# An mLSTM kernel with a gated MLP behind it: how the first four cells get their decay matrices, and the order of the head around it

## The chip, the cores and the metric

The kernel runs on one core of a Trainium2 chip. A core has a matrix engine (TensorE, PE in the profile; its weight loads are listed apart as PEld), a vector engine (VectorE, DVE), a scalar engine for activations (ScalarE, ACT), a general engine (GpSimd, POOL) and a queue that only issues transfers (SyncE, SP). Each takes its instructions in the written order and waits on semaphores for the others. The metric is the time of one execution in device microseconds (us), and less is better.

## The reference

The first block is an mLSTM cell: 4 batches by 8 heads, 768 steps, head size 40. Per step, with a running maximum `m` that keeps the exponentials in bounds:

```python
m_new = np.maximum(f_gate[:, :, t] + m, i_gate[:, :, t])
f_stab = np.exp(f_gate[:, :, t] + m - m_new)
i_stab = np.exp(i_gate[:, :, t] - m_new)
C = f_stab * C + i_stab * np.einsum('bhd,bhe->bhde', vt, kt)
n = f_stab * n + i_stab * kt
y[:, :, t] = sigmoid(o_gate) * (C @ qt) / np.maximum(np.abs(n @ qt), 1.0)
```

Its output (3072 rows of 320) goes through an MLP: `h = x @ w_in` (320 by 2048), `g = h * cos(h)`, `out = g @ w_out`. All inputs are float64 in memory, so the kernel also turns the bits of the weights into float32.

## The kernel before

**Tiling.** The sequence is cut into six chunks of 128 steps. One cell is one chunk of one batch (8 heads), so there are 24 cells; cell n is chunk n // 4 of batch n % 4. Within a cell the recurrence is done as attention: the scores of q and k are weighted with a decay matrix E[s, h, t] = exp(a_s - M_t), zero for s > t, where F is the running sum of the forget gates, a = i - F and M the running maximum of a. The weighted scores times the values give the outputs, and what the chunk leaves for later ones is added to a state. The MLP of a chunk (its four cells are its 512 columns) runs while the next chunk's cells are made.

**Stages.** `first_cells` is the head: the gates, cells 0 to 3, the gates of the other five chunks (32 rows by 640), and the preparation of cell 4 (B = 4). `first_period` starts the MLP of chunk 0 with `Up(0, 0)`: two weight rows of the first dimensions (L749) and the last 64 dimensions (`low`, L743), then scores and values of cell 4. After it the matrix engine has the MLP's products and one cell per period to the end. The order of all of it is written out by hand (`manual_schedule`): the calls in `first_cells` are the order of each engine's queue.

**A cell of the head.** `turn` transposes q and k on PE, `turn_out` copies them from PSUM on ACT, `scores` multiplies them, `weigh` multiplies the scores with E on DVE (two halves, L566), `values` multiplies with the values on PE, `normalize` divides on DVE (L650 to L658), `seam` transposes the result and makes the state's increment on PE, `seam_out` copies the transposed output (xT, L712) and `state` the increment (L724) on ACT.

**E in the head.** The maxima M are split into three bfloat16 parts (`maxima_in_parts`: five DVE instructions, L271 to L275, and one ACT copy) so that a bfloat16 product can spread them over all partitions. `maxima_in` puts into a PSUM bank a wall (1e30 where s > t, `wall_in`, L442, 128x512) and adds M with four products per half cell (`spread`, L449). `less_sums` subtracts a on DVE, in two halves per cell (L467), into E; `decay` takes exp(-E) on ACT (L472, 128x1024).

**The later gates.** `gates_sums` is a DVE scan over 640 columns (L290), `gates_less_sums` subtracts on POOL (L293 to L295), `gates_maxima` is the second DVE scan (L298) and sends M to memory from POOL's queue (L300, M_d), `gates_shifts` makes m0 on POOL (L304, L305). `gates_carry` takes five exponentials on ACT, one per chunk with the bias m0 (L309), and sends them from POOL's queue in two transfers (L312, G_d). `gates_exp` takes five more with the bias -M of the chunk's end (L316). `gates_turn` and `gates_turn_out` put a and these exponentials into a table by partition (`tab`).

**Weights.** `take_apart` (two ACT instructions, L175 and L177), `bound` (two on DVE, L181 and L182), `join` (DVE, L191) and `round_up` (POOL, L196) turn a piece of float64 bits into float32. Cell 4's E comes back from M_d (`load_M`, L436), is walled by POOL's `decay_exponents` (L462) and goes through eight exponentials (L476). `weigh_k` (POOL, L481) weights k for the state; `odd_constants` are four POOL memsets (L138, L139). `warm` (L1096) issues matmuls of zeros into a bank that nobody reads.

Of the kernel before, what the change touches and what calls it, by code (L numbers as in the profile page):

```python
# [29 lines left out]
def kernel(  # L30
# [57 lines left out]
    M0_parts = small[:, 704:768].bitcast(BF)  # L88
    of_parts = small[:, 768:784].bitcast(BF)
    nc.vector.memset(nil, 0.0)  # L90
    ident = const.tile([128, 128], FP, name="ident")
# [8 lines left out]
    nc.vector.memset(M0_parts, 0.0)  # L100
    nc.vector.memset(of_parts, 0.0)

    nc.gpsimd.memset(wall, 0.0)
# [163 lines left out]
    def maxima_in_parts():  # L267
# [8 lines left out]
        nc.scalar.copy(out=M0_parts[BH:2 * BH], in_=mid)  # L276

    def gates_first_out():
        pg = ps_o.tile([128, 2, BH], FP, name="pg", tag="o")
        for j, src in enumerate((a0, e0)):  # L280
            nc.tensor.transpose(pg[:, j], src, ident[0:BH, 0:BH])
        nc.vector.tensor_copy(out=tab[:, 0, 0:2], in_=pg)
# [24 lines left out]
    def gates_carry():  # L307
        for c in range(R):
            nc.scalar.activation(out=eG[:, c], in_=M1[:, c], func=AF.Exp, scale=-1.0, bias=m0[:, c:c + 1])  # L309
        dst = G_d.rearrange("(c j q) s -> j q c s", c=R, j=2)  # L310
        for j in range(2):
            nc.gpsimd.dma_start(out=dst[j], in_=eG[j:BH:2])  # L312

    def gates_exp():
        for c in range(R):
            nc.scalar.activation(out=eW[:, c], in_=a1[:, c], func=AF.Exp, bias=nM1[:, c:c + 1])  # L316

# [134 lines left out]
    def psum_o():  # L452
        return ps_o.tile([128, HP, C], FP, name="pm", tag="o")
# [15 lines left out]
    def decay(n, heads=range(H)):  # L469
        c, b = divmod(n, B)  # L470
        if n < B:
            nc.scalar.activation(out=Es[n], in_=Es[n], func=AF.Exp, scale=-1.0)  # L472
            return
# [634 lines left out]
    def first_cells():  # L1108
# [40 lines left out]
        turn_out(1, False)  # L1149
        weigh(0)  # L1150
        sigmoid_next()
        sigmoid(0)
        exp_next()
        gates_sums()
        gates_less_sums()
        values(0)
        pieces.extend(weights_in(0))
        scores(1)
        weigh(1)
        maxima_in(2)  # L1160
        less_sums(2)
        decay(2)
        values(1)
        normalize(0)
        normalize(1)
        maxima_in(3)
        less_sums(3)
        turn(2)
        turn_out(2, False)
        weigh_k(2)  # L1170
        seam(0)
        seam_out(0)
        scores(2)
        state(0)
        decay(3)
        weigh(2)
        seam(1)
        seam_out(1)
        weigh_k(3)
        gates_maxima()  # L1180
        gates_shifts()
        load_M(B)
        load_blocks(B)
        load(B, "kv")
        outs.append((0, weights_out(0)))
        turn(3)
        turn_out(3, False)
        values(2)
        normalize(2)
        state(1)  # L1190
# [43 lines left out]
        decay(B)  # L1234
        odd_constants()
        odd_values_of(B)
# [418 lines left out]
```

## Time and profile before

| what | us |
|---|---|
| median of 3 runs | 505.82 |
| lowest, highest | 504.16, 506.86 |
| the profiled execution | 503.72 |
| its span in the profile | 501.9 |
| PE busy | 495.1 |
| DVE busy | 420.6 |
| ACT busy | 332.5 |
| POOL busy | 300.0 |

A line of the timeline has the start in us from the span's start, the busy time, the engine, the line of the kernel, the operation with output and inputs, its shape, and a count; in brackets is the idle time before it and what ended that. A line by source shows the shortest, median and longest duration in ns.

### The profile page before, as it was taken

The page shows a single profiled execution, that of the slowest core. Times are in us where ns is not written, and L with a number is a line of the kernel's source. Part 1 is how long each engine was busy: PE and PEld are TensorE (multiplying, and loading weights), DVE is VectorE, ACT ScalarE, POOL GpSimd, SP SyncE. Part 2 cuts the span into 40 slices and gives each one's busy share as a digit, 9 for nine tenths or more (in the row PEclk, how much of TensorE's full clock was granted, in tenths as well). Part 3 has the DMA queues.
Part 4 walks back from the last instruction along what each step waited for, and adds up shares of the span by engine and source line. Part 5 has one row for each costly group of instructions (what it writes and reads, how often), then busy time and mean ns, then how long its engine had stood idle before and what let it go on. Part 6 is the DMA issues. An engine that isn't in the chain of part 4 may idle for free.

```text
span 501.9 us, 11143 instructions
## 1 busy us (share of the span) xinstructions
PE 495.1 (99%) x4038; PEld 375.4 (75%) x4038; DVE 420.6 (84%) x842; ACT 332.5 (66%) x646; POOL 300.0 (60%) x394
## 2 busy tenths in 40 slices
PE   9999999999999999999999999999999999999997
PEld 6856656565667668887887888788788888787876
DVE  7899998999878878899889889889979866777565
ACT  6799997878564575765877846777847743443541
POOL 8254557666555576787558877657567446434340
PEclk9999999999999999999999999999999999999999
DMA  9989899997366346129446118628113000010001
GB/s 139 182 223 239 213 224 279 233 217 136 114 178 111 101 120 127 50 86 202 132 125 106 48 54 195 168 83 150 43 35 85 1 7 5 2 54 0 2 0 54
DMA packets 100663, 56.74 MB, mean 113 GB/s; under 512 B 63456, under 2 KB 93360, under 8 KB 100608
## 3 DMA queue, kind: packets, MB, share of 16 engines
q1 hardware_dynamic: 97408, 54.43, 46.8%
q10 hardware_dynamic: 2896, 1.23, 1.0%
q8 instruction: 32, 0.52, 0.5%
q0 software_dynamic: 304, 0.36, 0.3%
q14 instruction: 23, 0.19, 0.1%
HBM read 50.66 MB, written 4.10 MB: 109 GB/s over the span
## 4 chain that ended last, share of the span: by engine, by line
PE 85%; ACT 4%; DVE 3%; DMA 2%; SPq 2%; POOL 2%; issue 1%; DVEq 0%; ACTq 0%; POOLq 0%
PE acc L1014 24%; PE pup L817 17%; PE pup L749 9%; PE po L863 6%; PE pup L833 6%; PE late L1014 5%; PE ps L560 4%; PE pup L743 3%; PE vt L595 2%; PE vt L586 2%; PE pu L701 2%; PE ph L576 1%; DMA E<-M_d 1%; DMA vs<-in_v_dram 1%; DVE n L760 1%
## 5 line engine op out<-in xcount | busy, mean ns | idle before, releaser
L757 ACT ACTIVATE n<-pup 128x512 int32<-128x512 f32 x64 | 37.0, 593 | 84.2 <-DVE pup L842 58.4
L765 ACT ACTIVATE n<-n 128x512 f32<-128x512 f32 x96 | 57.7, 626 | 16.5 <-DVE n L760 12.5
L852 POOL TENSOR_TENSOR g<-g,n 128x512 f32<-128x512 f32 x31 | 39.6, 1278 | 47.5 <-ACT n L765 47.4
L749 PE MATMUL pup<-xT,w_in_sb 128*128 128x512 f32 x128 | 58.7, 601 | 0.3 <-ACT xT L712 0.2
L1014 PE MATMUL acc<-w_out_sb,g 128*128 128x160 f32 x320 | 58.7, 303 | 0.0
L760 DVE SCALAR_TENSOR_TENSOR n<-pup,n 128x512 f32<-128x512 f32 x64 | 43.1, 689 | 18.5 <-ACT n L757 15.9
L834 POOL TENSOR_TENSOR blocks<-blocks 128x256 f32<-128x256 f32 x32 | 25.1, 785 | 54.5 <-ACT blocks L826 54.5
L1014 PE MATMUL acc<-T,g 128*128 128x160 f32 x304 | 56.4, 301 | 0.0
L817 PE MATMUL pup<-xT,w_in_sb 128*128 128x256 f32 x192 | 53.5, 385 | 0.2
L476 ACT ACTIVATE E<-E,tab 128x128 f32<-128x128 f32 x160 | 50.1, 389 | 4.3 <-POOL E L462 4.1
L1014 PEld LDWEIGHTS acc<-w_out_sb,g 128*128 128x128 f32 x320 | 49.0, 190 | 4.7 <-issue 2.7
L769 DVE TENSOR_TENSOR g<-pup,n 128x512 f32<-128x512 f32 x64 | 42.7, 687 | 5.7 <-ACT n L765 4.8
L1014 PEld LDWEIGHTS acc<-T,g 128*128 128x128 f32 x304 | 46.5, 190 | 1.1 <-issue 0.4
L749 PEld LDWEIGHTS pup<-xT,w_in_sb 128*128 128x128 f32 x128 | 23.1, 189 | 30.7 <-issue 30.0
L825 ACT COPY blocks<-pup 128x512 f32<-128x512 f32 x32 | 18.6, 582 | 34.2 <-PE pup L817 33.8
L817 PEld LDWEIGHTS pup<-xT,w_in_sb 128*128 128x128 f32 x192 | 33.8, 189 | 9.6 <-ACT blocks L826 4.4
L817 PE MATMUL pup<-x_room,room 128*128 128x256 f32 x128 | 38.5, 382 | 0.0
L542 POOL TENSOR_TENSOR qG<-t,G 128x512 f32<-128x512 f32 x20 | 26.4, 1321 | 16.7 <-DVE t L538 16.7
L1014 PE MATMUL acc<-T,blocks 128*128 128x160 f32 x160 | 36.2, 308 | 0.2 <-POOL blocks L904 0.2
L863 PE MATMUL po<-w_out_sb,g 128*128 128x320 f32 x128 | 36.2, 436 | 0.1
L833 PE MATMUL pup<-xL,w_in_l 64*128 64x512 f32 x128 | 36.1, 641 | 0.0
L566 DVE TENSOR_TENSOR E<-ps,E 128x512 f32<-128x512 f32 x46 | 29.5, 682 | 5.8 <-PE ps L560 5.6
(227 smaller groups left out, 1210.7 us busy)
## 6 DMA issues: line engine op xcount, KB each, us to landing
E<-M_d SPq DMA_DIRECT2D x20, 512.0 KB, 6.0
qr<-in_q_dram SPq DMA_DIRECT2D x72, 80.0 KB, 2.6
kr<-in_k_dram SPq DMA_DIRECT2D x72, 80.0 KB, 2.2
bits<-in_moe_w_out_dram SPq DMA_DIRECT2D x8, 640.0 KB, 6.2
G<-G_d SPq DMA_DIRECT2D x18, 256.0 KB, 5.7
blocks<-in_moe_w_in_dram SPq DMA_DIRECT2D x32, 128.0 KB, 4.6
out_dram<-o_sb SPq DMA_DIRECT2D x23, 160.0 KB, 1.8
o<-in_o_gate_dram SPq DMA_DIRECT2D x40, 80.0 KB, 4.4
```

Of the source, the lines that this page charges most:

```text
L476: nc.scalar.activation(out=Es[n][:, h], in_=Es[n][:, h], func=AF.Exp, scale=-1.0, bias=tab[:, c, 0, g:g + 1])
L566: nc.vector.tensor_tensor(out=w, in0=pss[n][j], in1=w, op=OP.mult)
L749: nc.tensor.matmul(pu.rearrange("p (b t) -> p b t", b=B), w_in_sb[:, i, ts(2 * f2 + e, 128)], xT[c][:, i:NK * B:NK], start=(i == 0 and not ...
L757: nc.scalar.activation(out=self.n[e], in_=self.pu[e], func=AF.Copy, bias=0.25)
L760: nc.vector.scalar_tensor_tensor(out=self.n[e].bitcast(FP), in0=self.pu[e], scalar=0.25, in1=self.n[e], op0=OP.add, op1=OP.subtract)
L765: nc.scalar.activation(out=r, in_=r, func=AF.Sin, scale=TWO_PI_DOWN)
L769: nc.vector.tensor_tensor(out=g, in0=self.pu[e], in1=self.n[e].bitcast(FP), op=OP.mult)
L817: nc.tensor.matmul(bank[:, part].rearrange("p (b t) -> p b t", b=B // 2), w[:, f2], x, start=start, stop=stop, skip_group_check=True)
L833: nc.tensor.matmul(pu, w_in_l[r, f2], xL[c][r].rearrange("p b t -> p (b t)"), start=False, stop=True, skip_group_check=True)
L852: tt(out=self.g, in0=self.g, in1=self.n[e].bitcast(FP), op=OP.mult)
L863: nc.tensor.matmul(po[c][b], gs[c, f][:, ts(b, C)], w_out_sb[:, f], start=(f == 0), stop=(f == NF - 1))
L1014: nc.tensor.matmul(a, lhs, rhs, start=start, stop=stop)
```

## The change

For cells 2 and 3 the DVE subtraction goes. A new `sums_in_parts` splits -a into three bfloat16 parts as M is split already, and `exponents_in` puts a into the bank by a product (128x512) in the place of the wall; M is added as before. ACT takes the exponential straight from PSUM in two halves, and POOL zeroes s > t behind it (128x1024). `gates_carry` and `gates_exp` become a POOL subtraction or addition over all 640 columns and one exponential each. The order of the head changes: `gates_maxima` ahead of `weigh(2)`, `scores(2)` and the turn of cell 3 ahead of `seam(1)`, the first `take_apart` ahead of `state(0)`, `values(2)` behind `scores(3)`, `load_M` of cell 4 behind four other loads, `odd_constants` early; two calls of `warm` (8 matmuls) go.

```diff
+    a0_parts = small[:, 784:848].bitcast(BF)
+    nc.vector.memset(a0_parts, 0.0)
...
+    def sums_in_parts():
+        rest, mid = blocks[0:BH, 38], blocks[0:BH, 39].bitcast(BF)[:, 0:C]
+        hi = a0_parts[0:BH]
+        nc.vector.tensor_scalar(out=hi, in0=a0, scalar1=-1.0, scalar2=None, op0=OP.mult)
+        nc.vector.scalar_tensor_tensor(out=rest, in0=a0, scalar=-1.0, in1=hi, op0=OP.mult, op1=OP.subtract)
+        nc.vector.tensor_copy(out=mid, in_=rest)
+        nc.vector.tensor_tensor(out=rest, in0=rest, in1=mid, op=OP.subtract)
+        nc.vector.tensor_copy(out=a0_parts[2 * BH:3 * BH], in_=rest)
+        nc.scalar.copy(out=a0_parts[BH:2 * BH], in_=mid)
+
+    def exponents_in(n):
+        for i in range(2):
+            m = pm[n, i] = psum_o()
+            g = n * H + HP * i
+            nc.tensor.matmul(m, a0_parts, of_parts[:, g:g + HP].unsqueeze(2).to_broadcast([128, HP, C]),
+                             start=True, stop=False)
+            spread(n, i)
...
     def gates_carry():
-        for c in range(R):
-            nc.scalar.activation(out=eG[:, c], in_=M1[:, c], func=AF.Exp, scale=-1.0, bias=m0[:, c:c + 1])
+        nc.gpsimd.tensor_tensor(out=eG, in0=m0.unsqueeze(2).to_broadcast([BH, R, C]), in1=M1, op=OP.subtract)
+        nc.scalar.activation(out=eG, in_=eG, func=AF.Exp)
...
     def gates_exp():
-        for c in range(R):
-            nc.scalar.activation(out=eW[:, c], in_=a1[:, c], func=AF.Exp, bias=nM1[:, c:c + 1])
+        nc.scalar.activation(out=eW, in_=eW, func=AF.Exp)
+
+    def gates_less_last():
+        nc.gpsimd.tensor_tensor(out=eW, in0=a1, in1=nM1.unsqueeze(2).to_broadcast([BH, R, C]), op=OP.add)
...
         if n < B:
-            nc.scalar.activation(out=Es[n], in_=Es[n], func=AF.Exp, scale=-1.0)
+            E = Es[n]
+            for i in range(2):
+                nc.scalar.activation(out=E[:, ts(i, HP)], in_=pm[n, i], func=AF.Exp, scale=-1.0)
+            nc.gpsimd.affine_select(out=E, in_=E, compare_op=OP.is_ge, fill=0.0, base=0,
+                                    pattern=[[0, H], [1, C]], channel_multiplier=-1)
             return
...
+        gates_sums()
         sigmoid_next()
+        sums_in_parts()
         sigmoid(0)
         exp_next()
-        gates_sums()
         gates_less_sums()
+        odd_constants()
         values(0)
         pieces.extend(weights_in(0))
         scores(1)
         weigh(1)
-        maxima_in(2)
-        less_sums(2)
+        exponents_in(2)
         decay(2)
         values(1)
         normalize(0)
         normalize(1)
-        maxima_in(3)
-        less_sums(3)
+        exponents_in(3)
+        gates_maxima()
+        gates_shifts()
         turn(2)
         turn_out(2, False)
         weigh_k(2)
+        decay(3)
         seam(0)
+        load_blocks(B)
+        load(B, "kv")
+        load_M(B)
+        outs.append((0, weights_out(0)))
+        scores(2)
         seam_out(0)
-        scores(2)
+        weigh(2)
+        turn(3)
+        turn_out(3, False)
+        take_apart(*pieces[0])
         state(0)
-        decay(3)
-        weigh(2)
         seam(1)
         seam_out(1)
         weigh_k(3)
...
         gates_carry()
+        gates_less_last()
         load_G_of(B)
...
         scores(3)
-        take_apart(*pieces[0])
-        seam(2)
+        bound(pieces[0][0])
+        state(1)
+        values(2)
         weigh(3)
-        bound(pieces[0][0])
-        seam_out(2)
-        gates_exp()
-        take_apart(*pieces[1])
-        warm(2, psum_o())
-        values(3)
         join(*pieces[0])
         round_up(*pieces.pop(0))
-        state(2)
+        gates_exp()
+        take_apart(*pieces[0])
+        normalize(2)
+        values(3)
         more = weights_in(1)
         pieces.append(next(more))
+        seam(2)
+        seam_out(2)
+        state(2)
         normalize(3)
-        warm(6, psum_o())
-        gates_turn(pg, 1)
...
         decay_exponents(B)
+        gates_turn(pg, 1)
         seam(3)
```

More of the change, by code (lines that the diff above doesn't have):

```diff
@@ L470, in decay @@
         c, b = divmod(n, B)
+        if n < 2:
+            nc.scalar.activation(out=Es[n], in_=Es[n], func=AF.Exp, scale=-1.0)
+            return
         if n < B:
-            nc.scalar.activation(out=Es[n], in_=Es[n], func=AF.Exp, scale=-1.0)
+            E = Es[n]
[3 more added lines that the diff above has]
+                                    pattern=[[0, H], [1, C]], channel_multiplier=-1)
             return
@@ L1179, in first_cells @@
         weigh_k(3)
[L1180 to L1190, printed above, removed]
         gates_carry()
+        gates_less_last()
         load_G_of(B)
@@ L1234, in first_cells @@
         decay(B)
-        odd_constants()
         odd_values_of(B)
```

## The prediction

> **What bounds the kernel now.** I read the page first, then each engine's timeline over the first 60 us, because every edit lies there.
>
> ```profile
> span 501.9 us, 11143 instructions
> ...
> PE 495.1 (99%) x4038; PEld 375.4 (75%) x4038; DVE 420.6 (84%) x842; ACT 332.5 (66%) x646; POOL 300.0 (60%) x394
> ...
> PE 85%; ACT 4%; DVE 3%; DMA 2%; SPq 2%; POOL 2%; issue 1%; DVEq 0%; ACTq 0%; POOLq 0%
> ```
>
> PE is busy nearly throughout and is 85% of the chain that ended last. The windows show how evenly: 69.93 of 70 us from 60 to 130, 224.99 of 225 from 130 to 355. There is no slack behind the head, so a head that ends later delays the end by as much. What counts is when the first MLP products (L749, L743) and the first evictions (L757) start.
>
> ```profile
> 28.65 1.47 PE L1096 MATMUL pm<-room 128*128 128x512 bf16 x6
> ...
> 31.89 3.67 PE L749 MATMUL pup<-xT,w_in_sb 128*128 128x512 f32 x8 [0.23 <-ACT xT L712]
> 36.11 1.13 PE L743 MATMUL pup<-xL,w_in_l 64*128 64x512 f32 x4 [0.56 <-POOL w_in_l L196]
> ...
> 24.74 1.57 ACT L309 ACTIVATE w_out_sb<-w_out_sb,m 32x128 f32<-32x128 f32 x5 [1.01 <-POOL m L304]
> 27.90 1.57 ACT L316 ACTIVATE w_out_sb<-w_out_sb,nM 32x128 f32<-32x128 f32 x5
> 29.37 0.66 ACT L175 ACTIVATE w_in_sb<-blocks 128x512 f32<-128x512 f32 x1
> 31.37 0.37 ACT L712 COPY xT<-px 128x256 f32<-128x256 f32 x1
> 37.29 1.08 ACT L757 ACTIVATE n<-pup 128x512 int32<-128x512 f32 x2
> ```
>
> L749 waits for ACT's last xT copy at 31.37, and from there to the eviction at 37.29 ACT has 5.92 us of work without a gap. So ACT's order, and what ACT waits for, sets the end of the head; the zero matmuls (L1096) only fill waits.
>
> ```profile
> 11.85 1.53 POOL L293 TENSOR_TENSOR w_out_sb<-w_out_sb 32x640 f32<-32x640 f32 x1
> 23.70 0.78 POOL L300 DMA_DIRECT2D M_d<-w_out_sb  x1 [1.65 <-DVE nM L303]
> 26.62 1.09 POOL L312 DMA_DIRECT2D G_d<-w_out_sb  x2 [1.76 <-ACT w_out_sb L309]
> 33.43 1.15 POOL L462 TENSOR_SCALAR_AFFINE_SELECT E<-E 128x1024 f32<-128x1024 f32 x1
> ...
> 10.10 1.68 DVE L290 TENSOR_TENSOR_SCAN w_out_sb<-w_out_sb 32x640 f32<-32x640 f32 x1
> 13.31 1.29 DVE L566 TENSOR_TENSOR E<-ps,E 128x512 f32<-128x512 f32 x2 [1.53 <-PE ps L560]
> 21.59 1.80 DVE L298 TENSOR_TENSOR_SCAN w_out_sb<-w_out_sb,blocks 32x640 f32<-32x640 f32 x1
> ...
> 450.12 1.42 POOL L852 TENSOR_TENSOR g<-g,n 128x512 f32<-128x512 f32 x1 [3.12 <-ACT n L765]
> ...
> 450.45 1.37 DVE L903 TENSOR_TENSOR g<-g 128x256 f32<-128x256 f32 x1
> ```
>
> POOL has the prices of what is added to it. The last pair matters most: L903 has two operands in SBUF and takes 0.42 us as a rule, but 1.37 when it starts inside a POOL operation. It ends 0.28 after POOL does, so it waited for POOL.
>
> **The change part by part.**
>
> *Work taken off.* DVE loses four half subtractions of 0.68 (0.60 start to start, 2.4 us). ACT loses ten exponentials of 0.39 (two rows of 1.57) and gets two of 32x640. Those lie between 0.66 (128x512, L175) and 0.78 (128x640, the same line later); I take 0.76, nearest in size. ACT saves 1.6. Reading E from PSUM in halves costs 2 x 0.59 (an ACT copy of 128x512 from PSUM) for 1.06, +0.12 a cell, beside ACT's idle 0.6 after it. PE's products stay in number and size (the wall's 128x512 becomes a's); it loses eight zero matmuls of 0.22 in waits: nothing on the path. One more DVE memset of 0.11 falls into the 0.54 that DVE waits for the gates.
>
> *The parts of a.* Five DVE instructions like L271 to L275 (0.36, 0.28, 0.27, 0.28, 0.22: 1.4 us) follow the scan L290, which ends at 11.78, and one ACT copy of 0.30. Unhindered they end at 13.2, just ahead of weigh(1) at 13.31: free. But POOL's L293 starts at 11.85 and its two copies end at 13.64. The first part is on its way by then; the second instruction reads two SBUF operands and by the L903 row waits until about 13.6. The parts are then ready at 14.6, and weigh(1) moves from 13.31 to 14.6. ACT's copy of the middle part, 14.2 to 14.5, stands ahead of the sigmoid (13.36), which moves by 1.1, and behind it a table load and decay(2), 16.05 to 17.1. [...]
>
> *Up to the maxima.* PE follows by 1.3: turn(2) 17.04 to 18.4, the transposes of cell 0 17.92 to 19.3 to 20.0. The last step of normalize(1) waits for them as now (18.72), to 20.1 and 20.6. The scan of the maxima then comes at once, with no subtraction and no weigh(2) ahead of it (2.4 us): 20.6 to 22.1, against 21.59 to 23.39. M_d leaves POOL at 22.1, 1.6 earlier. On SP, load_M stands behind four block loads and k and v (together 2.8 us of issue) and needs no wait for M_d (1.5 now). It goes out at about 27.9 instead of 26.70 and by its 6.7 us lands at 34.6; POOL's select of cell 4 comes later than that (36), so nothing.
>
> *POOL's queue, the new bound.* Behind M_d now stand, in this order: m0 (0.36), weigh_k(2) (0.70, before M_d until now), the select of cell 3 (1.12), weigh_k(3) (0.70) and the carry's subtraction (1.53, as L293). 22.1 + 0.8 + 0.36 + 0.70 + 1.12 + 0.70 + 1.53 = 27.3, and 0.3 for DVE's bound(), which interleaves there: 27.6. ACT has idled since its copies of cell 1 ended at 26.2. Its exponential runs to 28.4 (L309 ended at 26.3). Then the G_d transfers: 0.3 until issue (26.31 to 26.62 now) and 1.09, to 29.8; behind them gates_less_last, 1.53, to 31.3. Only then can ACT take the second exponential, 31.4 to 32.1, where L316 ended at 29.46. ACT waits some 2.2 us for it, with take_apart, cell 2's copies and cell 3's behind it.
>
> *From there.* take_apart 1.13, seam_out(2) 0.43 and state(2) 0.73 follow: the xT copy of cell 3 is at 34.4, +3.0 to 31.37. L749 starts at 34.9. The wait of 0.56 at L743 goes: POOL finishes w_in_l at about 38.3 and L749 at 38.6. ACT's 5.92 bring the eviction to 40.3, +3.0. The same sum on the old order puts xT at 31.7 for the 31.37 of the row, so I take off 0.3, and 0.2 for the L743 wait: **+2.5**.
>
> *The other line.* The first take_apart needs its fourth transfer, issued at 19.7 and 4.2 to landing: 23.9, so ACT waits there about 0.7. bound() starts at 24.6, meets POOL's select and weigh_k (each pair in that position, 32.44 and 33.66, took 1.1 an instruction instead of 0.3) and delays weigh(3), 25.54 now, to 26.4. normalize(2) now comes behind it, then normalize(3): its transposes end at 33.0, +1.4 to xT. So if POOL's line were shorter, this one ends last.
>
> *Covered.* odd_constants (1.25 on POOL) leaves 36.0 for 13.7, in POOL's idle stretch. scores(3) starts at 23.7 instead of 24.27, but weigh(3) is later anyway. values(2) fills PE meanwhile. G_d is 2 us later, so load_G_of waits on SP to about 33 (32.39 now) and lands by 38; scale_q needs it at 39.
>
> Sum: the profiled time 503.72 + 2.5 = 506.2 (span 504.4). The runs' median lies 2.1 above the profiled execution, so against the runs: 505.8 + 2.5 = **508.3**.
>
> **The rivals.**
>
> *Not slower: the second exponential is in time.* The place is ACT's wait behind gates_less_last. It decides nothing if POOL is through with it by 28.3 (31.37 less the 2.29 of ACT work behind and the 0.76 itself). That needs 3 us less on POOL: the parts unhindered (1.3) and the issue of G_d beside the subtraction (1.4), and DVE's bound() not held up on the other line. For it: a transfer's issue is not counted as busy, so it may leave POOL free. Against: L304 started at 24.50, when the M_d row (23.70, 0.78) was over. Then ACT's savings show, xT moves by 0 to -0.6 and the time is 505.3.
>
> *POOL is slower than its rows.* A subtraction that reads a stride-zero operand, and a select over a tile that ACT has just written, stand in no row of this size. With 2.2 for each subtraction and 1.5 for each select xT moves by 4.2: 510.
>
> *The matrix clock drops.* In the first 3.66 us of the span nine 128x512 bfloat16 matmuls take 0.43 each start to start; later ones, with the granted clock at 1.00, take 0.22. The fillers go, and on my schedule PE waits up to 1.5 us (13.2 to 14.7, for the parts) and 1.4 (31.0 to 32.3, for the second exponential). If that halves the clock over L749, its 3.67 us double: 512. The longest gap in the trace of before is 0.56, so it can't exclude this. [...]
>
> **How the numbers follow.** About 0.5% (2.5 us) is what a measurement of this kernel can tell from no change, and my sum lies on that bound. Forecast, 507 to 509.3: 0.55. Not slower, 504.5 to 506.5: 0.22. Slower POOL, 509.3 to 511: 0.15. Clock: 0.05. A gain past 0.5% that I can't name: 0.03. The range leaves out the clock, the gain and the outer ends: 505.0 to 510.6. Within 0.5%: 0.22 and half of the forecast, 0.50. Slower: the other half, POOL and clock, 0.47.
>
> **What would show it.** The second DVE instruction of the parts lasting about 1.6 us. The M_d issue near 22. The second gate exponential on ACT as one row near 31.4, with idle time before it put down to POOL. The first L749 near 34.9 and the first L757 near 40. If the exponential comes by 28.5, or L749 before 32, I am wrong, and the head was bounded by ACT's work. If L743 starts more than 4 us behind L749, the clock fell.

## The result and the profile after

The changed kernel takes 510.94 us (median of 10 executions, 507.33 to 512.20), the kernel before beside it on the same chip 504.49 (504.00 to 506.86). The ratio is 1.0104, with a 95% interval from 1.0075 to 1.0133: slower by about 1%. The profiled execution of the changed kernel took 511.46, with a span of 509.7, 7.8 us over the span before.

The change renumbers the kernel. The first MLP products, L749 and L743 before, are now L780 and L774; the first eviction L757 is L788; `values` is L607; the last step of `normalize` is L689; the parts of a are made in L284 to L289 and used in L296. The two gate exponentials are L331 and L337, and GpSimd's passes ahead of them L330 and L340.

First the page of the changed kernel; its third line gives TensorE's granted clock in 40 slices of 12.7 us, in tenths of full speed.

```profile
span 509.7 us, 11125 instructions
...
PE 499.9 (98%) x4030; PEld 380.4 (75%) x4030; DVE 423.4 (83%) x844; ACT 331.6 (65%) x641; POOL 305.5 (60%) x398
...
PEclk9588999999999999999999999999999999999999
...
PE 85%; DVE 4%; ACT 3%; POOL 2%; SPq 2%; DMA 2%; issue 1%; DVEq 0%; ACTq 0%; POOLq 0%
```

TensorE still carries 85% of the chain, and from the fifth slice on the clock digits are all nines. The second to fourth, from 12.7 to 51 us, are 5, 8 and 8: in the head the matmuls ran at half clock for part of the time. The windows say when; the last columns are the granted clock, the share of the DMA engines and the bytes moved.

```profile
10.00:15.00 5.00, 3.44 (x36) 3.23 (x36) 4.86 (x7) 3.00 (x6) 4.89 (x11) 0.95 1.25 170
15.00:20.00 5.00, 4.76 (x25) 4.24 (x26) 2.75 (x9) 3.53 (x5) 1.31 (x3) 0.50 1.43 144
20.00:25.00 5.00, 5.00 (x41) 4.10 (x42) 0.95 (x5) 1.66 (x4) 0.00 (x0) 0.53 0.87 215
...
30.00:35.00 5.00, 4.08 (x34) 3.63 (x33) 4.86 (x11) 1.75 (x7) 3.91 (x6) 0.99 0.84 228
35.00:40.00 5.00, 3.99 (x48) 3.35 (x49) 4.11 (x11) 3.75 (x12) 2.92 (x3) 0.50 0.39 136
```

In the kernel before each of these windows has 1.00. Here the trace's record of the clock has two falls to one half, from 14.46 to 24.70 and from 34.94 to 41.76. From 20 to 25 us TensorE is busy for all 5 us and does 41 instructions; before, the same window holds 65:

```profile
20.00:25.00 5.00, 5.00 (x65) 4.65 (x65) 4.49 (x10) 3.45 (x10) 1.86 (x4) 1.00 0.94 224
```

Next the timeline around the waits that the prediction spoke of:

```profile
15.24 0.59 PE L296 MATMUL pm<-room 128*128 128x512 bf16 x1 [1.69 <-DVE room L288]
31.98 1.95 PE L607 MATMUL ph<-vs,blocks 128*128 128x41 f32 x16 [0.29 <-issue]
34.46 0.44 PE L723 MATMUL px<-ident,y 128*128 128x128 f32 x2 [0.53 <-DVE y L689]
36.01 0.69 PE L725 MATMUL px<-ident,y 128*64 128x128 f32 x4 [1.12 <-DVE y L689]
39.83 4.64 PE L780 MATMUL pup<-xT,w_in_sb 128*128 128x512 f32 x8
44.40 1.13 PE L774 MATMUL pup<-xL,w_in_l 64*128 64x512 f32 x4
...
12.31 1.55 DVE L285 SCALAR_TENSOR_TENSOR blocks<-blocks,room 32x128 f32<-32x128 f32 x1
33.98 1.98 DVE L689 TENSOR_TENSOR y<-room,dn 128x256 f32<-128x256 f32 x2
...
32.42 0.74 ACT L331 ACTIVATE w_out_sb<-w_out_sb 32x640 f32<-32x640 f32 x1 [2.03 <-POOL w_out_sb L330]
35.90 0.74 ACT L337 ACTIVATE w_out_sb<-w_out_sb 32x640 f32<-32x640 f32 x1 [2.11 <-POOL w_out_sb L340]
45.56 1.08 ACT L788 ACTIVATE n<-pup 128x512 int32<-128x512 f32 x2 [0.36 <-PE pup L774]
...
12.19 1.52 POOL L315 TENSOR_TENSOR w_out_sb<-w_out_sb 32x640 f32<-32x640 f32 x1
27.26 0.79 POOL L322 DMA_DIRECT2D M_d<-w_out_sb  x1 [7.53 <-DVE nM L325]
34.59 1.27 POOL L340 TENSOR_TENSOR w_out_sb<-w_out_sb,nM 32x640 f32<-32x640 f32 x1
```

Both things are there. VectorE's L285 lasts 1.55 us beside GpSimd's L315, TensorE waits 1.69 for the parts, and ScalarE waits 2.03 and 2.11 for GpSimd ahead of the two exponentials: these are the waits foretold. But the first MLP product starts at 39.83, not at 34.9, because between 14.46 and 24.70 TensorE's matmuls take up to about twice as long (the 16 products of L607 3.58 us at 16.90 and 1.88 at 10.58), and then again from 34.94 on; L774 follows L780 after 4.57 us, where it takes 3.60 at full clock (36.55 to 40.15 in the first experiment).

### The profile page after: what moved, and what is told of

The parts are those of the page before. It is cut to its first block, busy times and chain, and to the rows that moved or that the text cites. A ratio compares the mean times of both kernels' runs of the same rounds, so it can differ in the third digit from the quotient of the medians.

```text
span 509.7 us, 11125 instructions
## 1 busy us (share of the span) xinstructions
PE 499.9 (98%) x4030; PEld 380.4 (75%) x4030; DVE 423.4 (83%) x844; ACT 331.6 (65%) x641; POOL 305.5 (60%) x398
## 4 chain that ended last, share of the span: by engine, by line
PE 85%; DVE 4%; ACT 3%; POOL 2%; SPq 2%; DMA 2%; issue 1%; DVEq 0%; ACTq 0%; POOLq 0%
PE acc L1045 25%; PE pup L848 18%; PE pup L780 9%; PE pup L864 6%; PE po L894 6%; PE late L1045 4%; PE ps L591 4%; PE pup L774 3%; PE vt L626 2%; PE vt L617 2%; PE pu L732 1%; DMA E<-M_d 1%; DVE n L791 1%; PE vt L620 1%; PE vt L623 1%
## 5 line engine op out<-in xcount | busy, mean ns | idle before, releaser
L788 ACT ACTIVATE n<-pup 128x512 int32<-128x512 f32 x64 | 37.1, 593 | 84.9 <-DVE pup L873 58.7
L780 PE MATMUL pup<-xT,w_in_sb 128*128 128x512 f32 x128 | 59.6, 609 | 0.0
L780 PEld LDWEIGHTS pup<-xT,w_in_sb 128*128 128x128 f32 x128 | 23.5, 193 | 30.6 <-issue 30.3
L873 DVE TENSOR_TENSOR pup<-pup,blocks 128x256 f32<-128x256 f32 x32 | 13.9, 434 | 24.0 <-PE pup L864 23.7
```

The lines of the kernel that those rows point to most:

```text
L780: nc.tensor.matmul(pu.rearrange("p (b t) -> p b t", b=B), w_in_sb[:, i, ts(2 * f2 + e, 128)], xT[c][:, i:NK * B:NK], start=(i == 0 and not ...
L788: nc.scalar.activation(out=self.n[e], in_=self.pu[e], func=AF.Copy, bias=0.25)
```

## The experiments

Two theories stood against each other about the 6.4 us that the change costs against the 504.49 beside it. **Waits**: they are the waits for GpSimd and the longer order. **Clock**: the waits are worth about 2.5 us as summed, and the rest is half clock, which the change brings because TensorE is left with too little to do at some places. A third, **GpSimd beside VectorE**, came up on the way: VectorE's instructions take longer beside what GpSimd was given (L285 1.55 us beside L315, and 0.28 in parts_first, where L315 comes later).

For the comparison of kernels at equal clock I use the executions whose mean granted clock is 0.998 or more, and set them against the executions of the kernel before that ran beside them, under the same condition. Of the kernel before 97 of the 113 that ran beside the experiments are such; the other 16 show 0.996 or 0.997, so it too loses some clock now and then. Of the changed kernel none of 10 is: 0.983 to 0.993.

### Fillers where TensorE waits

```diff
         scores(1)
+        warm(8)
         weigh(1)
...
         values(3)
+        idle = psum_o()
+        warm(4, idle)
...
         decay_exponents(B)
+        warm(6, idle)
         gates_turn(pg, 1)
```

> The changed kernel with 18 zero matmuls (128x512, 0.22 us each at the full clock) put where PE waited: eight behind scores(1), four behind values(3), six ahead of the second turn of the gates. Theory C (the clock): in the changed kernel PE's waits let the granted clock fall to half twice (10.24 and 6.83 us), and that is all of the loss beyond the 2.5 us of the forecast's waits; filled, the mean clock is 1.000, the first L780 starts near 35 instead of 39.8, and the time is 2.5 us over the kernel before (ratio 1.005). Theory W (waits alone): the clock only shows what the waits did, PE has slack in the head, and the fillers change nothing: L780 near 39.8, ratio 1.010 to 1.013.

Measured: 507.65 (506.55 to 508.41), ratio 1.0049 [1.0027, 1.0071]. Half of the loss is gone with nothing but zeros added. In the profiled execution the clock fell once, from 30.19 to 33.60. Three of ten executions held it (506.55, 507.32 and 507.59): 507.15 on average against 504.21 before, +2.9. The mean clock of 1.000 and the L780 near 35 that the clock theory had expected were not reached; L780 starts at 36.55.

```profile
12.64 1.60 DVE L285 SCALAR_TENSOR_TENSOR blocks<-blocks,room 32x128 f32<-32x128 f32 x1
...
28.29 0.74 ACT L331 ACTIVATE w_out_sb<-w_out_sb 32x640 f32<-32x640 f32 x1 [1.87 <-POOL w_out_sb L330]
31.76 0.74 ACT L337 ACTIVATE w_out_sb<-w_out_sb 32x640 f32<-32x640 f32 x1 [2.10 <-POOL w_out_sb L340]
36.03 0.37 ACT L743 COPY xT<-px 128x256 f32<-128x256 f32 x1 [1.21 <-PE px L725]
...
36.55 3.67 PE L780 MATMUL pup<-xT,w_in_sb 128*128 128x512 f32 x8 [0.22 <-ACT xT L743]
```

The waits for GpSimd are all still there, about as long as in the changed kernel (1.87 and 2.10 for 2.03 and 2.11); so it was the clock that gave 3.3 us back. The six fillers ahead of the turn were more than the gap: ScalarE's last copy now waits 1.21 for TensorE.

### The parts ahead of the scan

```diff
-        gates_sums()
         sigmoid_next()
         sums_in_parts()
+        gates_sums()
```

> The changed kernel with the five DVE instructions of the parts ahead of the scan of gates_sums, so that they are through before POOL starts its subtraction of 1.53 us. The second of them should take 0.28 us instead of 1.55, and PE should not wait 1.69 us for the parts. Theory C: the first stretch at half clock (14.5 to 24.7) goes and with it 3 us or more, and the second may stay; ratio 1.003 to 1.008. [...]

Measured: 507.97 (506.45 to 510.85), ratio 1.0057 [1.0030, 1.0083]. With the scan behind the parts, GpSimd's subtraction comes later too, and the second instruction takes 0.28. The first fall is gone; the clock falls later, at 27.42, for 10.24 us, while TensorE waits ahead of the values of cell 3.

```profile
11.60 0.28 DVE L285 SCALAR_TENSOR_TENSOR blocks<-blocks,room 32x128 f32<-32x128 f32 x1
...
27.99 3.61 PE L607 MATMUL ph<-vs,blocks 128*128 128x41 f32 x16 [1.71 <-ACT w_out_sb L331]
```

### The kernel before without its eight fillers

```diff
-        warm(2, psum_o())
         values(3)
...
         normalize(3)
-        warm(6, psum_o())
```

> The kernel before without its eight zero matmuls behind weigh(3) and normalize(3), and nothing else changed. If taking away the fillers is what lets the clock fall, the granted clock halves somewhere from 28 to 38 and the time is 2 to 4 us longer (ratio 1.004 to 1.008). If the waits that the change makes are what does it, PE idles about 1.8 us there in pieces under 1 us, the mean clock stays 1.000 and the time stays (ratio 0.999 to 1.001).

Measured: 506.73 (504.48 to 508.78), ratio 1.0029 [1.0003, 1.0054], clock 0.992 to 0.996 in all ten. Nothing differs from the kernel before but these matmuls and the two PSUM banks that they took, so half clock is the likely whole of what this loses: 2.5 us by the medians, 1.5 by the ratio. The fall at 35.44 is in L749:

```profile
33.80 0.44 PE L692 MATMUL px<-ident,y 128*128 128x128 f32 x2 [0.68 <-DVE y L658]
34.16 0.44 PE L694 MATMUL px<-ident,y 128*64 128x128 f32 x4
34.43 0.51 PE L701 MATMUL pu<-vs,kw 128*40 128x48 f32 x16
35.16 5.37 PE L749 MATMUL pup<-xT,w_in_sb 128*128 128x512 f32 x8 [0.22 <-ACT xT L712]
```

The longest wait ahead of that fall is 0.68 us, and eight matmuls that took 3.67 take 5.37. This execution had another fall, from 18.37 to 21.79, behind a wait of 1.84 for the values of cell 1 to land. That wait is earlier than the fillers and is not theirs, so the loss is an upper bound for what the fillers are worth.

### The ten gate exponentials back in the changed kernel

```diff
-        nc.gpsimd.tensor_tensor(out=eG, in0=m0.unsqueeze(2).to_broadcast([BH, R, C]), in1=M1, op=OP.subtract)
-        nc.scalar.activation(out=eG, in_=eG, func=AF.Exp)
+        for c in range(R):
+            nc.scalar.activation(out=eG[:, c], in_=M1[:, c], func=AF.Exp, scale=-1.0, bias=m0[:, c:c + 1])
...
-        nc.scalar.activation(out=eW, in_=eW, func=AF.Exp)
+        for c in range(R):
+            nc.scalar.activation(out=eW[:, c], in_=a1[:, c], func=AF.Exp, bias=nM1[:, c:c + 1])
...
-        gates_less_last()
```

> The changed kernel with the ten short exponentials of the gates back on ACT and both of POOL's additions to them gone. ACT should no longer wait 2.03 and 2.11 us for POOL. By the forecast's second line (bound behind the weights' landing, then two normalizations) the last xT copy then comes 1.1 us earlier and no more, so at most 1.1 us less than the changed kernel where the clock goes the same way; the first stretch at half clock stays, since the parts are as late as before. Theory W: ratio 1.007 to 1.011. Theory C: the same first stretch, the second one may go, since PE waits less there; ratio 1.005 to 1.011.

Measured: 510.20 (507.47 to 511.59), ratio 1.0106 [1.0078, 1.0134]. No gain: the clock falls as often (0.983 to 0.993), and TensorE waits 1.90 for the normalization of cell 2 in place of the gates. No gate pass is left on GpSimd, and the last step of that normalization (L690) still takes 1.93: it lies beside GpSimd's `round_up` of the weights (L198, 29.54 to 30.84). What the gate part costs can only be read where the clock holds (below).

### One part alone in the kernel before: the second exponential

```diff
         gates_shifts()
+        gates_less_last()
...
-        for c in range(R):
-            nc.scalar.activation(out=eW[:, c], in_=a1[:, c], func=AF.Exp, bias=nM1[:, c:c + 1])
+        nc.scalar.activation(out=eW, in_=eW, func=AF.Exp)
```

> The kernel before with one part of the change alone: the second gate exponential (five of 0.31 us on ScalarE, 1.57 in all) becomes one of 0.74, and GpSimd adds the 32x640 shift for it (1.27) right behind the cells' maxima, where in the trace of before it waits 1.76 for ScalarE. Theory (the exponential itself is a gain, and what was lost in the change is where GpSimd's addition stood, behind the DMAs): 0.5 to 0.8 us less than before, no half clock. [...] Rival (any new gap of TensorE brings the half clock): 506 to 507, with the granted clock below 0.997 in all runs.

Measured: 505.63 (504.44 to 510.33), ratio 1.0033 [1.0007, 1.0059]. My theory fell: there is no gain from one exponential for five here, even with GpSimd's addition in a place where GpSimd had waited.

```profile
24.88 1.24 POOL L318 TENSOR_TENSOR w_out_sb<-w_out_sb,nM 32x640 f32<-32x640 f32 x1
...
25.02 1.54 DVE L660 TENSOR_TENSOR y<-room,dn 128x256 f32<-128x256 f32 x2
...
26.48 0.69 PE L694 MATMUL px<-ident,y 128*128 128x128 f32 x2 [0.97 <-DVE y L660]
```

The last step of cell 2's normalization takes 1.54 beside the addition, and TensorE waits 0.97 for it. In the kernel before it takes 0.56:

```profile
24.95 0.56 DVE L658 TENSOR_TENSOR y<-room,dn 128x256 f32<-128x256 f32 x2
```

At the end of TensorE's wait the clock fell in the profiled execution, from 26.48 to 29.90, and in 5 of 12 executions. The seven others average 504.93 against 504.48 before. These +0.5 fit the stretched step, but they are within the scatter of the seven (504.44 to 506.14); the rest of the loss is the clock's.

### The other part alone: products and masks

```diff
         sigmoid_next()
+        sums_in_parts()
...
-        maxima_in(2)
-        less_sums(2)
+        exponents_in(2)
...
-        maxima_in(3)
-        less_sums(3)
+        exponents_in(3)
```

with `decay` as in the change.

> The kernel before with the other part alone: the sums of cells 2 and 3 are subtracted by products, the parts of a are made behind the sigmoid, GpSimd masks behind the exponential; the order of the rest is that of before, and the gate exponentials are the ten of before. Theory (the parts, by their second instruction's wait for GpSimd, hold the weighing of cell 1 and make a gap on TensorE): a gap of 1 to 1.7 us on TensorE near 13 to 16 us, VectorE's two 1.28 us subtractions gone behind it, so at full clock between 504 and 505.5; with the half clock that such a gap brought in the changed kernel 506 to 508. Rival (this part is free, the loss is the order of the rest and the exponentials): 504.2 within 0.4, the clock full.

Measured: 505.29 (504.35 to 506.15), the clock full in 12 of 12; the kernel before 504.47. The ratio, 1.0005 [0.9988, 1.0022], shows no difference; at equal clock it is 505.26 against 504.48, +0.8. The row that fits it is the values of cell 1, which wait for a weighing that the parts hold up:

```profile
15.31 1.98 PE L605 MATMUL ph<-vs,E 128*128 128x41 f32 x16 [0.56 <-DVE E L595]
```

They start at 15.31 for 14.38 before. In this profile the delay goes on down the line: M_d leaves at 24.93 for 23.70, and the last xT copy is at 32.48 for 31.37. So the replacement of VectorE's subtractions costs little, and gains nothing although VectorE does 2.4 us less. A likely reason, argued and not tried: in the kernel before, TensorE's waits from the values of cell 1 to the first MLP product are 0.23 us and what the eight fillers cover (1.84 by their starts), and those lie behind cell 2's and cell 3's normalization, where the subtractions are long over.

### Clock held, parts first, GpSimd's addition ahead of the DMAs of G

```diff
     def gates_carry():
         nc.gpsimd.tensor_tensor(out=eG, in0=m0.unsqueeze(2).to_broadcast([BH, R, C]), in1=M1, op=OP.subtract)
+        gates_less_last()
         nc.scalar.activation(out=eG, in_=eG, func=AF.Exp)
...
-        gates_less_last()
         load_G_of(B)
...
-        warm(6, idle)
+        warm(3, idle)
```

(against the kernel with fillers, without its first eight, and with the parts ahead of the scan)

> The changed kernel with three edits: parts ahead of the gates' scan, GpSimd's second addition ahead of the DMAs of G (it waits 1.70 for ScalarE there), and seven fillers where TensorE stood idle (four ahead of normalize(3), three ahead of the second turn). Theory (loss = waits for GpSimd plus half clock): ScalarE's second wait of 2.10 goes, the eviction's start comes 1 to 1.5 us earlier than in the kernel with fillers alone, 505.3 to 506.3 where the clock holds. Rival (the line through the landing of the second expert weights and the conversion bounds anyway): 506.5 to 507 at full clock, ScalarE's wait gone without a gain. Rival (the half clock comes all the same): 507 to 508.

Measured: 508.67 (505.98 to 509.07), ratio 1.0064 [1.0037, 1.0090]. The clock held in two of eight, 506.42 on average, +1.9.

```profile
30.76 0.44 PE L724 MATMUL px<-ident,y 128*128 128x128 f32 x2 [1.53 <-DVE y L690]
...
28.24 0.74 ACT L338 ACTIVATE w_out_sb<-w_out_sb 32x640 f32<-32x640 f32 x1
...
26.83 1.75 DVE L193 SCALAR_TENSOR_TENSOR w_in_sb<-blocks,w_in_sb 128x512 int32<-128x512 int32 x1
...
26.79 1.25 POOL L341 TENSOR_TENSOR w_out_sb<-w_out_sb,nM 32x640 f32<-32x640 f32 x1
```

ScalarE's wait of 2.10 is gone, and the loss is less, though the parts and the fillers moved too and only two executions (505.98 and 506.86) tell. TensorE still waits. In this place the addition lies beside L193, which takes 1.75 instead of 0.69, and the normalization behind it (L690, 1.36 for 0.56) then lies beside `round_up` (L198, 29.11 to 30.41).

### The same with the weighing of cell 3 ahead of the conversions

```diff
-        bound(pieces[0][0])
         state(1)
         values(2)
         weigh(3)
+        bound(pieces[0][0])
```

> As the one before it in this call, and the first two conversions of the second expert weights stand behind the weighing of cell 3 on VectorE instead of ahead of it. Theory (the weights land near 25 us, and the weighing waits behind them for nothing): TensorE's values of cell 3 begin 1 to 2 us earlier, no gap of 1.71 there, 504.5 to 505.5 where the clock holds. Rival (the conversion, GpSimd's carry of 1.3 us and the product of the weights are the longer line): TensorE's values begin earlier, and the first product of the experts does not; time as in the run before it, within 0.4.

Measured: 507.74 (506.06 to 510.31), ratio 1.0062 [1.0041, 1.0083]; the clock held in 4 of 12, 506.42 on average, the same as the run before. The values of cell 3 start at 26.48 for 26.41, so they gain nothing either, as there was no gap of 1.71 left in the run before (0.28 there, 0.39 here). The time is unchanged, as the rival had it, but not for the rival's reason.

### The ten exponentials back, clock held

(against the kernel with GpSimd's addition ahead of the DMAs of G, two headings up)

```diff
     def gates_carry():
-        nc.gpsimd.tensor_tensor(out=eG, in0=m0.unsqueeze(2).to_broadcast([BH, R, C]), in1=M1, op=OP.subtract)
-        gates_less_last()
-        nc.scalar.activation(out=eG, in_=eG, func=AF.Exp)
+        for c in range(R):
+            nc.scalar.activation(out=eG[:, c], in_=M1[:, c], func=AF.Exp, scale=-1.0, bias=m0[:, c:c + 1])
...
     def gates_exp():
-        nc.scalar.activation(out=eW, in_=eW, func=AF.Exp)
+        for c in range(R):
+            nc.scalar.activation(out=eW[:, c], in_=a1[:, c], func=AF.Exp, bias=nM1[:, c:c + 1])
```

> As held, with the ten gate exponentials of before in place of GpSimd's two passes and the two exponentials. Theory (GpSimd's passes stretch VectorE's conversions and normalization beside them, 1.75 for 0.69 and 1.36 for 0.56, and that is worth more than the 1.7 us which ScalarE saves): these two back near 0.7 and 0.6, TensorE's wait of 1.53 ahead of cell 2's turn goes, 505.2 to 506.0 where the clock holds. Rival (ScalarE's 1.7 us more bind here): ScalarE without a wait from the carry on, TensorE's gap as long, 506.4 to 507.2 where the clock holds. In both the clock falls in fewer runs if the gap is under 0.6, in most if it is over 1.

Measured: 506.54 (505.06 to 507.95), ratio 1.0040 [1.0025, 1.0056]; the clock held in 5 of 12, 505.69 on average, +1.4 against the kernel before, where the two passes had +1.9. In this profile L193 and the normalization are back:

```profile
27.06 0.68 DVE L193 SCALAR_TENSOR_TENSOR w_in_sb<-blocks,w_in_sb 128x512 int32<-128x512 int32 x1
28.64 0.56 DVE L690 TENSOR_TENSOR y<-room,dn 128x256 f32<-128x256 f32 x2
...
24.09 1.98 PE L608 MATMUL ph<-vs,E 128*128 128x41 f32 x16
26.80 3.29 PE L608 MATMUL ph<-vs,blocks 128*128 128x41 f32 x16 [0.73 <-ACT xL L748]
```

Beside GpSimd's pass (1.25) and its `round_up` (1.30) L193 and the normalization took 1.75 and 1.36 in held; with neither beside them they take 0.68 and 0.56 here. What that is worth in time is not shown: 0.6 us between 2 and 5 executions is within their scatter. The passes are not the only ones beside which VectorE takes longer either, as the next kernel's profile tells. And the clock fell, at 27.22, behind a wait of only 0.73. That led to the next question.

### What the clock goes by

In the changed kernel's trace the clock's record has 10.24 us at half clock, 10.24 at full, 6.83 at half and 467.63 at full: 3, 3, 2 and 137 times 3.413. In the kernel before it has 498.35 at full, 146 times. I lay a grid of 3.41 us through the changes in each profile; counted from the span's start its phase differs (14.46 is 0.80 past a multiple of 3.413 in the changed kernel, 30.19 is 2.88 past one in fillers). In the 14 profiles of this case there are 128 such stretches between about 7 and 46 us that run at full clock; 11 of them end in a fall. I gave each matmul its columns out of 128 as a weight (a 128x41 product counts 0.32 of its busy time, anything of 128 columns or more counts in full) and summed per stretch. The busy times are those of the timeline.

| stretch | TensorE without a row | weighted load | behind it |
|---|---|---|---|
| fillers, 26.78 to 30.19 | 0.28 us | 1.38 us | half clock |
| changed kernel, 11.04 to 14.46 | 0.91 | 1.59 | half |
| changed kernel, 31.52 to 34.94 | 0.86 | 1.12 | half |
| held_old, 23.81 to 27.22 | 0.73 | 1.10 | half |
| parts_scan (below), 18.17 to 21.59 | 1.32 | 1.92 | full |
| held, 29.49 to 32.91 | 1.26 | 1.79 | full |
| kernel before, lowest load | 0.00 | 1.99 | full |

All 11 falls follow a load of 1.59 us or less out of 3.41. Of the 117 stretches without a fall two have so little (1.48 and 1.55, both in old_gates), and two more lie just above (1.62 in held, 1.66 in old_gates), so the edge is not a sharp one. The weighting is a choice made after these falls; it sorts the stretches and does not explain the clock. Idle time alone sorts them badly: 0.28 to 1.89 before a fall, up to 1.32 without. Ten of the 11 thin stretches hold a part of a `values`: sixteen 128x41 products that take TensorE 1.9 us by the rows and, so weighted, load it for 0.6. The other one (no_warm, 32.03 to 35.44) has waits and the 32x32 and 128x48 products ahead of L749. The changed kernel sets the values of cells 2 and 3 next to each other and takes away the fillers that stood there.

The test of it: four fillers between the two, in the kernel with the clock held and the ten exponentials.

```diff
         normalize(2)
+        idle = psum_o()
+        warm(4, idle)
         values(3)
-        idle = psum_o()
         warm(4, idle)
```

> As held_old, with four more matmuls of zeros (128x512, 0.22 each) between the values of cell 2 and those of cell 3, where TensorE waited 0.73. Theory (the clock falls behind a stretch of 3.41 us in which the matmuls, each counted by its columns out of 128, keep TensorE loaded for less than about 1.6 us; in held_old that stretch, 23.81 to 27.22, had 1.10, and the fillers add 0.9): the clock holds in 9 or more of 12 runs, where it held in 5 of 12, values of cell 3 at most 0.3 later, median 505.2 to 505.9. Rival (single idle gaps do not decide, and narrow products alone do not either; the falls here come from something else): the clock falls in 5 or more of 12, median 506.2 or more.

Measured: 505.93 (505.26 to 506.86), ratio 1.0016 [1.0002, 1.0031]; the clock held in 11 of 12. The executions at full clock average 505.91 against 504.61, +1.3, as in held_old; what the four matmuls removed is the half clock. They also close TensorE's wait there, from 0.73 to 0.18, so this run alone does not tell load from idle time. The table does: the stretch with 0.28 us idle fell, those with 1.26 and 1.32 did not.

```profile
24.62 1.98 PE L608 MATMUL ph<-vs,E 128*128 128x41 f32 x16
26.77 1.02 PE L1128 MATMUL pm<-room 128*128 128x512 bf16 x4 [0.18 <-ACT xL L748]
27.64 1.88 PE L608 MATMUL ph<-vs,blocks 128*128 128x41 f32 x16
...
28.98 2.04 DVE L690 TENSOR_TENSOR y<-room,dn 128x256 f32<-128x256 f32 x2
...
29.62 1.30 POOL L198 TENSOR_TENSOR w_in_sb<-w_in_sb,blocks 128x512 int32<-128x512 int32 x1
```

The gate exponentials are the ten of before here too, and yet the normalization of cell 2 takes 2.04: it starts 0.34 later than in held_old's profile and meets `round_up`, which it had escaped there.

### Two other places for the parts

Behind the weighing of cell 1, with the scan of the maxima ahead of the weighing of cell 2 (against parts_only):

```diff
         sigmoid_next()
-        sums_in_parts()
...
         weigh(1)
+        sums_in_parts()
+        values(1)
         exponents_in(2)
         decay(2)
-        values(1)
...
         exponents_in(3)
+        gates_maxima()
+        gates_shifts()
...
         weigh_k(3)
-        gates_maxima()
-        gates_shifts()
```

> The kernel before with the products' part alone, as in parts_only, in another place: the three parts of a are made behind the weighing of cell 1 instead of ahead of the gates' scan, and the scan of the cells' maxima, with GpSimd's shifts behind it, stands ahead of the weighing of cell 2. Theory (the part costs only the 0.56 us by which it holds TensorE at cell 1, and what VectorE saves behind it can be spent on the carry): no gap over 0.3 us on TensorE at cell 1, the carry's exponentials some 2 us earlier than the 24.74 of before, the first product of the experts 0.3 to 1 us earlier than 31.89, the time 503.4 to 504.3. Rival (VectorE ahead of the normalizations is what matters, or the second expert weights land too late to use it): 504.4 to 505.5. Rival (GpSimd's masks beside VectorE's scans stretch them, the earlier carry is lost again): 504.4 to 505, the scan longer than 1.9.

Measured: 507.86 (506.45 to 508.13), ratio 1.0060 [1.0038, 1.0082], the clock below 0.997 in all six. A miss: I had not seen that the products of cell 2 had filled TensorE's wait for the values of cell 1 to land.

```profile
14.55 2.14 PE L605 MATMUL ph<-vs,E 128*128 128x41 f32 x16 [0.98 <-DMA vs<-in_v_dram]
```

And in parts_only, with the gates' scan moved behind the weighing of cell 1:

```diff
         exp_next()
-        gates_sums()
-        gates_less_sums()
...
         weigh(1)
+        gates_sums()
+        gates_less_sums()
         exponents_in(2)
```

> As parts_only, with the gates' scan, and GpSimd's subtraction that it releases, behind the weighing of cell 1 instead of between the parts and it. Theory (what the products' part costs at full clock is that parts and scan together stand ahead of the weighing of cell 1): TensorE's gap of 0.56 ahead of the values of cell 1 falls under 0.3, the first product of the experts comes 0.4 to 0.8 us earlier than in parts_only, and the time is 0.4 to 0.8 us under that kernel's 505.29, so within 0.4 of the kernel before; the clock stays full. Rival (the scan delays the normalization of cell 0, on which the turn waits): the gap goes, a new one ahead of the turn of cell 0, 505.0 to 505.6. Rival (the products and masks cost it themselves): no gap at all, and 505.2 or more.

Measured: 506.14 (505.50 to 507.95), ratio 1.0021 [1.0004, 1.0038], the clock full in 12 of 12. The gap of 0.56 went, as my theory had it, and the time rose: +1.6 at equal clock against +0.8 in parts_only. The new gap is where the first rival put it, ahead of the turn of cell 0's result, but through another cause and larger:

```profile
17.44 2.42 DVE L687 TENSOR_TENSOR y<-room,dn 128x256 f32<-128x256 f32 x2
...
16.62 1.53 POOL L315 TENSOR_TENSOR w_out_sb<-w_out_sb 32x640 f32<-32x640 f32 x1 [4.07 <-DVE dn L679]
18.36 1.08 POOL L500 TENSOR_SCALAR_AFFINE_SELECT E<-E 128x1024 f32<-128x1024 f32 x1
...
19.78 0.44 PE L721 MATMUL px<-ident,y 128*128 128x128 f32 x2 [1.31 <-DVE y L687]
```

GpSimd's subtraction and then its mask lie beside the two halves of cell 0's normalization: 2.42 us instead of 0.56. TensorE waits 1.31, and the clock stays full; by the weights above the stretch has 1.92, with wide matmuls on both sides of the wait.

No version with a part of the change was faster than the kernel before.

## Why the prediction was right or wrong

The forecast was 508.3 with a range up to 510.6; the median is 510.94, 2.6 above the figure and 0.3 outside the range. As a step from the kernel before the miss is larger: +2.5 forecast, +6.45 measured. The forecast stood on a median of three runs, 505.82, and ten runs of that kernel have 504.49; that the figure comes as near as 2.6 is partly luck. Of the sides no change had 0.50 and slower 0.47; slower it is, at 1.0104.

**Parts of a: right.** VectorE's second instruction 1.55 for about 1.6. The weighing of cell 1 began at 15.12 for 14.6; the scan ahead (1.94 for 1.68) and L286 (0.57 for 0.27) add up to the difference, and why they took longer is not shown. As in the row of L903, VectorE's instruction began inside a GpSimd pass and ended behind it: L285 0.15 us behind L315 (13.86 and 13.71), L660 of one_exp 0.44 behind the addition, L193 of held 0.54; in parts_scan L687 began inside the subtraction, and its first half ended 0.28 behind the mask that followed. L689 of the changed kernel is another case: its second half begins at 34.32, GpSimd's L340 only at 34.59, and yet it is VectorE that takes longer, to 35.96, 0.10 behind L340.

**Up to the maxima: right at full clock, overrun by the half clock.** M_d was to leave at 22.1; it left at 27.26, and at 23.14 in the kernel with fillers, whose weighing of cell 0 is 0.84 later than in the changed kernel's profile (9.81 for 8.97).

**GpSimd's queue: right.** From M_d to the end of the carry's subtraction 5.2 predicted, 5.13 measured (27.26 to 32.39); ScalarE's waits 2.03 and 2.11 for 1.4 and 2.2. The step's words were too narrow, though: a pass on GpSimd had not only its place in the queue, VectorE's instruction beside it also took longer (1.98 for 0.56 at L689, beside L340 and its 1.27). Whether the passes themselves cost time at full clock is open: held_old, without them, is at +1.4 and held at +1.9, within their scatter.

**The other line, +1.4: right in size.** It was said to end last if GpSimd's were shorter. With GpSimd's passes gone, held_old is at +1.4 and held_load at +1.3. In held_load's profile the weighing of cell 3 starts at 26.21 for 26.4, but the normalization behind it meets `round_up` (2.04 for 0.56), which this line did not have; so part of the agreement may be chance.

**The net of +2.5: right for the waits, wrong as the whole.** At held clock the change with fillers is at +2.9 (three executions), of which up to 1.2 may be fillers too many.

**The clock rival is the step that failed.** Its gaps were seen (1.5 and 1.4; measured 1.69, and 0.53 with 1.12), its time of 512 is near, its sign (L743 over 4 us behind L749) came, 4.57. But it had a chance of 0.05, and that gaps of 1.5 us cost nothing is shown by no run: the clock held behind a wait of 1.53 (held) and fell behind one of 0.73 (held_old). Idle time alone does not decide either: the clock fell with 0.28 us idle in the stretch (fillers) and held with 1.32 (parts_scan). What the profile has are two falls of the clock, 10.24 and 6.83 us long, where the sum had none, behind stretches that are thin, not idle (weighted loads of 1.59 and 1.12 of 3.41 us); the rival had one in mind, over L749, and the first began at 14.46 already. My estimate of the time it cost is the difference between 510.94 and the 507.15 of the kernel with fillers at full clock, 3.8, and up to 1.2 more if those fillers cost time themselves. It came in all ten executions.

I had also written that the eight lost fillers cost "nothing on the path". no_warm prices them at 2.5 us on the median (506.73 against 504.21) and 1.5 by the ratio, with a fall in it that may not be theirs.

**The other rivals.** Not slower: wrong, the second exponential did wait. Slower GpSimd, 510: wrong although near in time, for the passes took 1.43 and 1.27 and the selects 1.08 to 1.09, all under the sum's 1.53 and 1.12.

What stays open: the +0.6 between held_old and parts_only (order of the rest, or the parts' later scan of M) wasn't taken apart; nor what the stretched instructions are worth at full clock; nor what exactly the clock counts, since two stretches don't fit the weighted load and no run varied the width of the products alone.

## What to carry to other kernels

Matmuls of zeros beside a run of narrow products were not spare work here: without its eight the kernel before took 506.73 for 504.21 (no_warm, with the fall in it that may not be theirs). Before taking such away, or moving two narrow runs together, add up for each stretch of 3.41 us, the grid of the clock's records here, what it loads TensorE with, by columns and not by busy time alone. All falls came at 1.59 or less, and the profile of the kernel before has 1.99 in its thinnest stretch. Work that goes from ScalarE to GpSimd can be paid on VectorE too, where an instruction of two operands in SBUF lies beside it: here 1.2 to 1.5 us of GpSimd cost one such instruction 1.0 to 1.4 us in each of four places (L285 and L689 of the changed kernel, L660 of one_exp, L193 of held). It is not only those: L183 of the changed kernel, with one tensor operand, takes 1.74 beside the weighing of k and the mask, and 0.41 when it comes again at 37.45. An engine that does less need not gain anything where another one, here TensorE from cell 1 on, has almost no waits; that reason was argued here and not tried.

## What the runs showed of the hardware that I had not expected

- TensorE's clock halved behind a stretch in which TensorE was busy for 3.1 of 3.41 us by its rows, most of it with 128x41 products (fillers, 26.78 to 30.19); and it held through a stretch with 1.32 us of idle time (parts_scan, 18.17 to 21.59).
- Half clock lasted 3.41, 6.83 or 10.24 us, one to three stretches of the grid; the phase of the grid differs between the profiles (0.80 in the changed kernel, 2.88 in fillers), and that may be why one kernel has several times, which no run shows: the changed kernel 507.33 to 508.53 in the four executions at 0.990 or more, 510.75 to 512.20 in the six below.
- VectorE's product of two operands took longer beside GpSimd's mask (an affine select of 128x1024, 1.08), as beside GpSimd's additions: 2.42 for 0.56 beside a subtraction and a mask in a row (parts_scan). The first half of that product ends at 19.72, 0.28 after the mask and 1.57 after the subtraction.
